# An expert's largest weight over the partitions: two small TensorE products and a VectorE maximum in place of a POOL instruction

## The chip, the cores and the metric

The kernel runs on one core of a Trainium2 chip. The metric is the device time of one execution in microseconds. Before the change three runs gave 1509.94, 1512.34 and 1515.03 us; the median is 1512.34 us. One more execution was profiled; all rows below come from it.

## The reference

A batch of 8 sequences of 2496 tokens with 256 channels goes through a spectral filter and then through a mixture of eight experts, of which each token uses the one with the largest logit:

```python
X = np.fft.rfft(x, axis=1)
y = np.fft.irfft(X * F[None], n=x.shape[1], axis=1)      # F = filt_r + 1j * filt_i
x = y.reshape(B * S, D)                                   # 19968 tokens
xn = x / (np.linalg.norm(x, axis=-1, keepdims=True) + 1e-06)
en = expert_emb / (np.linalg.norm(expert_emb, axis=-1, keepdims=True) + 1e-06)
logits = xn @ en.T / tau
expert_idx = np.argmax(logits, axis=1)                    # and gate_w, its softmax weight
for e in range(E):
    mask = expert_idx == e
    h = np.maximum(x[mask] @ w1[e], 0.0)                  # 256 -> 1024
    out[mask] = gate_w[mask, None] * (h @ w2[e])          # 1024 -> 256
```

## The kernel before

Each of the eight sequences is one group. Its filter is a two-step Fourier transform written as products on TensorE. `conv_s1` (names `in`, `s`) multiplies the loaded tokens, scratch `SD` in DRAM takes the result; `conv_s2` loads it back (`a`), transforms (`s`), multiplies by the filter (`yy` and `xs` on VectorE, lines 458 and 460), adds the two on POOL (line 494, from the second group on) and transforms back (`sa`), into scratch `ZD`; `conv_sb` loads `ZD`, makes the tokens (`y`), turns them into two half-precision parts (`rows`), transposes them (`tp`), takes the logits (`lp`), and routes. Routing works on chunks of four steps (eight 128-row pieces; the last chunk of a group has six): VectorE finds the expert, TensorE counts the rows ahead (`rk`, line 682), VectorE makes the target indices (`ixi`, line 704), and POOL scatters each piece to its expert's area of `XS` (line 711, one indirect DMA a piece, 22 pieces a group).

An expert's block of 256 rows (a slot) loads its rows transposed (`xT`, line 834, on SP's queue), multiplies them by the expert's first weights (`ph`, line 865), makes `h` on ScalarE and VectorE (lines 871 and 872), multiplies by the second weights (`po`, line 892), and scatters the result (line 900, POOL). A slot of group g can start only when all 22 pieces of group g are scattered. Eight slots, one an expert, are run for each group while the next group's filter runs between their products; in the end 33 blocks of 128 rows take the rows that are left.

The weights are prepared once, while the first group's filter runs: for each expert e and each of its two matrices, VectorE takes the largest absolute value of each partition (`largest`, lines 239 to 243, name `wmax`), POOL spreads the maximum over the partitions (`spread_max`, line 246, name `wall`), VectorE turns it into a power of two (`scales`, lines 248 to 257, name `wsc`), and ScalarE, VectorE and POOL split the scaled weights into two half-precision parts (`halves`, lines 259 to 272; POOL's part is line 269). Experts 0 to 6 take both matrices in one call, expert 7 takes them in two calls, since its raw weights lie where expert 6's were: nine calls of `spread_max` in all. `prep` steps this work: 0.6 of a step for each step of the first group (`PREP_AT`, `PREP_RATE`), and one for each call of `spread` after that.

What sets the order: in the first group (the head, everything up to the first slot) TensorE's and ScalarE's instructions stand in the order of the code. A scheduler orders all the others, and everything behind the head, by its own timeline; each engine then runs its list strictly in order. The small tiles of TensorE's results share pools: `ps_c` has two buffers, which `s`, `sa`, `tp` and `rk` take in turn.

Of the kernel before, what the change touches and what calls it, by code (L numbers as in the profile page):

```python
# [13 lines left out]
F32 = mybir.dt.float32  # L14
F32R = mybir.dt.float32r
I32 = mybir.dt.int32
AF = mybir.ActivationFunctionType
ALU = mybir.AluOpType
AX = mybir.AxisListType
# [4 lines left out]
P = 128  # L24
# [7 lines left out]
E = 8  # L32
# [24 lines left out]
def moe_spectral_kernel(  # L57
# [16 lines left out]
    nc = tc.nc  # L74
# [12 lines left out]
    const = ctx.enter_context(tc.tile_pool(name="const", bufs=1))  # L87
# [14 lines left out]
    ps_c = ctx.enter_context(tc.tile_pool(name="ps_c", bufs=2, space=PSUM))  # L102
# [18 lines left out]
    ident = const.tile([P, P], F16, tag="ident", name="ident")  # L121
# [2 lines left out]
    nc.vector.tensor_copy(lt16, lt32)  # L124
    one16 = const.tile([P, P], F16, tag="one16", name="one16")
    nc.vector.memset(one16, 1.0)


    w8i = const.tile([P, E], I32, tag="w8i", name="w8i")
# [66 lines left out]
    isc = const.tile([P, E], F32, tag="isc", name="isc")  # L196

    wmax = const.tile([P, E, 2], F32, tag="wmax", name="wmax")
    wall = const.tile([P, E, 2], F32, tag="wall", name="wall")
    wsc = const.tile([P, E, 2], F32, tag="wsc", name="wsc")  # L200
    winv = const.tile([P, E, 2], F32, tag="winv", name="winv")
    wmx = const.tile([P, 4], F32, tag="wmx", name="wmx")
# [2 lines left out]
    def weight_load(q, e, j):  # L205

        w = (w1, w2)[j]
        if e + 1 < E:
            raw = W32[:, e + 1, j * 2048:(j + 1) * 2048]
            q.dma_start(raw, w[:, e])  # L210
            raws[e, j] = [[raw[:, i * 1024:(i + 1) * 1024]] for i in range(2)]
        elif j == 0:
            raw = W32[:, e, 2048:4096]
            q.dma_start(raw, w[:, e])
            raws[e, j] = [[raw[:, i * 1024:(i + 1) * 1024]] for i in range(2)]
        else:
            raw = W32[:, e, 2048:3072]
            q.dma_start(raw, w[:, e, 1024:2048])
            small = []
            for i in range(2):  # L220
                t = mp2.tile([P, 512], F32, tag="wp", name=f"wraw{i}")
                q.dma_start(t, w[:, e, i * 512:(i + 1) * 512])
                small.append(t)
            raws[e, j] = [small, [raw]]
# [10 lines left out]
    def weight_halves():  # L235

        v = nc.vector

        def largest(e, j):
            pieces = raws[e, j][0] + raws[e, j][1]  # L240
            for i, r in enumerate(pieces):
                v.tensor_reduce(out=wmx[:, i:i + 1], in_=r, axis=AX.X, op=ALU.max, apply_absolute_value=True)
            v.tensor_reduce(out=wmax[:, e, j:j + 1], in_=wmx[:, :len(pieces)], axis=AX.X, op=ALU.max)

        def spread_max(e, js):
            nc.gpsimd.partition_all_reduce(wall[:, e, js], wmax[:, e, js], P, bass.bass_isa.ReduceOp.max)

        def scales(e, js):
            v.tensor_scalar(out=wall[:, e, js], in0=wall[:, e, js], scalar1=2.0 ** -100, scalar2=None, op0=ALU.max)
            v.tensor_scalar(out=wsc[:, e, js].bitcast(I32), in0=wall[:, e, js].bitcast(I32), scalar1=0x7F800000,  # L250
                            scalar2=0x7F800000, op0=ALU.bitwise_and, op1=ALU.bitwise_xor)
            for j in range(js.start, js.stop):
                v.tensor_scalar(out=wsc[:, e, j:j + 1], in0=wsc[:, e, j:j + 1], scalar1=2.0 ** (13 if j else 5),
                                scalar2=None, op0=ALU.mult)
            v.reciprocal(winv[:, e, js], wsc[:, e, js])
            if js.stop == 2:
                v.tensor_tensor(out=isc[:, e:e + 1], in0=winv[:, e, 0:1], in1=winv[:, e, 1:2], op=ALU.mult)

        def halves(e, j):
            sc = wsc[:, e, j // 2:j // 2 + 1]  # L260
            pieces = raws[e, j // 2][j % 2]
            w = 1024 // len(pieces)
            for i, raw in enumerate(pieces):
                hi = W[:, e, j * 2048 + i * w:j * 2048 + (i + 1) * w]
                lo = W[:, e, j * 2048 + 1024 + i * w:j * 2048 + 1024 + (i + 1) * w]
                if j == 0:
                    nc.scalar.activation(raw, raw, AF.Copy, scale=sc)
                    nc.scalar.copy(hi, raw)
                    nc.gpsimd.tensor_tensor(out=lo, in0=raw, in1=hi, op=ALU.subtract)
                else:  # L270
                    nc.scalar.activation(hi, raw, AF.Copy, scale=sc)
                    v.scalar_tensor_tensor(out=lo, in0=raw, scalar=sc, in1=hi, op0=ALU.mult, op1=ALU.subtract)

        def maxima(e):
            for j in range(2):
                largest(e, j)
                if j:
                    spread_max(e, slice(0, 2))
                yield

        yield from maxima(0)
        for e in range(E - 1):
            if e + 1 < E - 1:
                yield from maxima(e + 1)
            scales(e, slice(0, 2))
            for j in range(4):
                halves(e, j)
                if j == 3:
                    prepped[0] = e + 1
                yield  # L290
        e = E - 1
        for j, order in ((0, (0, 1)), (1, (3, 2))):
            yield
            weight_load(nc.sync, e, j)
            yield
            yield
            largest(e, j)
            spread_max(e, slice(j, j + 1))
            yield
            scales(e, slice(j, j + 1))  # L300
            for k in order:
                halves(e, k)
                yield
        prepped[0] = E
# [800 lines left out]
```

## Time and profile before

| what | value |
|---|---|
| three runs, median | 1512.34 us (1509.94 to 1515.03) |
| profiled execution | 1499.08 us |
| its span, first to last instruction | 1497.2 us |
| mean granted TensorE clock, as a share of 2.4 GHz | 0.924 |
| busy: TensorE | 1301.8 us, 87% |
| busy: VectorE, ScalarE, POOL | 873.5, 693.7, 548.7 us |
| the nine POOL reductions | 3.3 us busy |

Busy time says how long instructions ran on an engine, not whether anybody waited for it. The span is 1.9 us shorter than the execution's own time. The profiled execution is 13 us (0.9%) faster than the median of the three runs, so a sum made in it is carried over as a difference.

### The profile page before, as it was taken

What the parts mean: (1) busy time and instruction counts of PE and PEld (TensorE: products, weight loads), DVE (VectorE), ACT (ScalarE), POOL (GpSimd) and SP (SyncE); (2) the same over time, 40 slices, a digit from 0 to 9 for tenths busy, and PEclk for the clock granted to TensorE, in tenths of its full rate; (3) what the DMA queues carried; (4) which work ended last, traced back from release to release, by engine and by line L of the source; (5) the groups of instructions that cost most, each with busy time, mean ns of one, the idle gap of its engine ahead of it and who ended that gap; (6) DMA issues with size and microseconds to landing.
All of it is one profiled execution on the core that took longest, in us unless ns stands there. A gap on an engine that the chain in (4) does not pass through costs nothing.

```text
span 1497.2 us, 31982 instructions
## 1 busy us (share of the span) xinstructions
PE 1301.8 (87%) x10956; PEld 988.2 (66%) x10956; DVE 873.5 (58%) x2841; ACT 693.7 (46%) x1578; POOL 548.7 (37%) x614
## 2 busy tenths in 40 slices
PE   5644557998997998899979988997999789999997
PEld 1212235766765776686658666865787578899997
DVE  2558765563474757575648555664658432266664
ACT  2435554543562665375437634662665122333332
POOL 0021454245524543552445254525433431222222
PEclk7876678999998999999989999999999889999999
DMA  8865375646774775577457746674753222122211
GB/s 273 302 213 200 118 211 158 187 133 189 215 188 130 205 217 156 166 220 183 140 166 201 195 121 185 195 192 124 200 169 92 76 67 54 50 49 48 49 45 40
DMA packets 230494, 229.16 MB, mean 153 GB/s; under 512 B 126089, under 2 KB 172497, under 8 KB 228405
## 3 DMA queue, kind: packets, MB, share of 16 engines
q1 hardware_dynamic: 200908, 151.93, 37.7%
q0 software_dynamic: 26400, 60.07, 12.8%
q10 hardware_dynamic: 3017, 15.02, 3.0%
q8 instruction: 92, 1.51, 0.4%
q14 instruction: 77, 0.63, 0.1%
HBM read 121.61 MB, written 84.84 MB: 138 GB/s over the span
## 4 chain that ended last, share of the span: by engine, by line
PE 61%; issue 15%; POOL 3%; DMA 2%; ACT 1%; DVE 1%; another core or an unknown queue 1%; POOLq 0%; SPq 0%; ACTq 0%; DVEq 0%
PE po L892 22%; PE ph L865 21%; PE y L403 5%; PE s L403 5%; POOL out_dram L900 3%; PE tp L606 2%; PE sa L408 2%; PE s L408 2%; DMA f<-ZD 1%; PE lp L621 1%; PE sa L512 1%; DMA ZD<-z 1%; DVE xs L460 0%; DMA f<-in_filt 0%
## 5 line engine op out<-in xcount | busy, mean ns | idle before, releaser
L892 PE MATMUL po<-W,h 128*128 128x256 f16 (+1 forms) x3864 | 519.8, 279 | 27.9 <-issue 27.5
L892 PEld LDWEIGHTS <-h 128*128 128x128 f16 x3864 | 375.5, 100 | 132.4 <-issue 85.3
L865 PE MATMUL ph<-xT,W 128*128 128x256 f16 x3072 | 414.8, 279 | 30.9 <-issue 18.7
L872 DVE SCALAR_TENSOR_TENSOR h<-ph,h 128x512 f16<-128x512 f32 (+1 forms) x388 | 232.0, 598 | 277.6 <-ACT h L871 240.6
L865 PEld LDWEIGHTS <-W 128*128 128x128 f16 x3072 | 300.1, 100 | 129.0 <-issue 91.4
L871 ACT ACTIVATE h<-ph 128x512 f16<-128x512 f32 (+1 forms) x388 | 203.4, 525 | 378.8 <-PE ph L865 205.4
L900 POOL DMA_INDIRECT out_dram<-o,meta x161 | 171.5, 1065 | 359.0 <-ACT o L899 319.4
L711 POOL DMA_INDIRECT XS<-rows,ixi x176 | 176.6, 1004 | 172.4 <-issue 136.2
L403 PE MATMUL y<-f,csb_sb 120*128 120x512 f32 (+1 forms) x192 | 101.2, 612 | 39.8 <-DVE rows L562 17.7
L494 POOL TENSOR_TENSOR yy<-yy,xs 128x512 f32<-128x512 f32 x70 | 94.3, 1349 | 109.1 <-DVE xs L460 69.5
L363 POOL DMA_DIRECT2D in<-in_x x84 | 66.9, 797 | 154.9 <-PE s L403 113.4
L403 PE MATMUL s<-in,c_sb 117*128 117x512 f32 (+1 forms) x192 | 111.1, 672 | 12.8 <-DMA in<-in_x 8.1
L865 PE MATMUL ph<-xT,wp 128*128 128x128 f16 x1584 | 104.9, 219 | 0.2
L865 PEld LDWEIGHTS <-wp 128*128 128x128 f16 x1584 | 96.7, 98 | 3.2 <-issue 0.7
L587 ACT ACTIVATE rows<-y 128x256 f16<-128x256 f32 x176 | 66.0, 384 | 64.7 <-PE y L403 58.8
L559 ACT ACTIVATE rows<-y,rr 128x256 f16<-128x256 f32 x176 | 73.9, 473 | 46.8 <-DVE rr L592 44.7
L426 ACT COPY s<-s 128x512 f32<-128x512 f32 x88 | 51.5, 586 | 91.4 <-PE s L403 43.5
L458 DVE TENSOR_TENSOR yy<-s,f 128x256 f32<-128x256 f32 x160 | 60.9, 419 | 52.5 <-ACT xs L487 39.4
L562 DVE SCALAR_TENSOR_TENSOR rows<-y,rr,rows 128x256 f16<-128x256 f32 x176 | 77.1, 478 | 22.5 <-ACT rows L559 19.8
L853 DVE COPY wp<-W 128x1024 f16 x132 | 62.1, 471 | 45.3 <-PE ph L865 44.8
L899 ACT ACTIVATE o<-po,meta 128x256 f32<-128x256 f32 x161 | 69.4, 475 | 34.2 <-PE po L892 26.7
L460 DVE SCALAR_TENSOR_TENSOR xs<-xs,sgn_sb,f 128x256 f32<-128x256 f32 x160 | 82.0, 551 | 0.0
(170 smaller groups left out, 1397.0 us busy)
## 6 DMA issues: line engine op xcount, KB each, us to landing
f<-in_filt SPq DMA_DIRECT2D x160, 256.0 KB
a<-SD SPq DMA_DIRECT2D x80, 256.0 KB
ZD<-z SPq DMA_DIRECT2D x80, 256.0 KB
SD<-s SPq DMA_DIRECT2D x80, 240.0 KB
f<-ZD SPq DMA_DIRECT2D x80, 240.0 KB
in<-in_x POOLq DMA_DIRECT2D x70, 234.0 KB
W<-in_w ACTq DMA_DIRECT2D x14, 1024.0 KB
XS<-rows,ixi POOLq DMA_INDIRECT x176
```

The source lines that it names most:

```text
L403: nc.tensor.matmul(out_, c[:a.shape[0]], a, start=True, stop=True)
L460: nc.vector.scalar_tensor_tensor(out=o, in0=i, scalar=sgn_sb[:, k2:k2 + 1], in1=f, op0=ALU.mult, op1=ALU.mult)
L494: nc.gpsimd.tensor_tensor(out=yy, in0=yy, in1=xs, op=ALU.add)
L559: nc.scalar.activation(rows[:, i, 0:D], y[:, i], AF.Copy, scale=rr[:, u:u + 1])
L562: nc.vector.scalar_tensor_tensor(out=rows[:, i, D:2 * D], in0=y[:, i], scalar=rr[:, u:u + 1], in1=rows[:, i, 0:D], op0=ALU.mult, op1=ALU.s ...
L711: i = nc.gpsimd.indirect_dma_start(out=XS, out_offset=bass.IndirectOffsetOnAxis(ap=ix, axis=0), in_=src, in_offset=None)
L865: last["pe"] = nc.tensor.matmul(ph[:, fi, :size], wp[:, k * 2 + wh, fi * P:(fi + 1) * P], xT[:, xh * 2 + k], start=(c == 0), stop=(c == 5))
L871: nc.scalar.activation(h[:, 0, :, :size], ph[:, :, :size], AF.Relu)
L872: hd = nc.vector.scalar_tensor_tensor(out=h[:, 1, :, :size], in0=ph[:, :, :size], scalar=0.0, in1=h[:, 0, :, :size], op0=ALU.max, op1=ALU. ...
L892: nc.tensor.matmul(self.po[:, s], self.hs[fp][:, hh, fi, s * P:(s + 1) * P], self.Wp[:, off + wh * 1024:off + wh * 1024 + D], start=(fp == ...
L899: nc.scalar.activation(o, self.po[:, s], AF.Copy, scale=self.meta[:, s, 1:2])
L900: i = nc.gpsimd.indirect_dma_start(out=out, out_offset=bass.IndirectOffsetOnAxis(ap=self.meta[:, s, 0:1].bitcast(I32), axis=0), in_=o, in_ ...
```

## The change

`spread_max` no longer uses POOL. VectorE first bounds the per-partition maxima from below and masks them to their exponents (these two steps stood in `scales` before). TensorE multiplies them by a 128x128 identity, which lays the 128 partitions' values along one row in a PSUM tile `pm`; VectorE takes the maximum of that row (`wtop`) and puts it on a 2x2 diagonal (`wdg`); a second product with a matrix of ones brings it to all 128 partitions, and VectorE flips the exponent into the scale `wsc`. The tile `pm` comes from the pool `ps_c`. Two constants, `ident32` and `one32`, are made at the start.

```diff
+    ident32 = const.tile([P, P], F32, tag="ident32", name="ident32")
+    nc.vector.tensor_copy(ident32, ident)
+    one32 = const.tile([2, P], F32, tag="one32", name="one32")
+    nc.vector.memset(one32, 1.0)
...
         def spread_max(e, js):
-            nc.gpsimd.partition_all_reduce(wall[:, e, js], wmax[:, e, js], P, bass.bass_isa.ReduceOp.max)
+
+            n = js.stop - js.start
+            m = wmax[:, e, js]
+            v.tensor_scalar(out=m, in0=m, scalar1=2.0 ** -100, scalar2=None, op0=ALU.max)
+            v.tensor_scalar(out=m.bitcast(I32), in0=m.bitcast(I32), scalar1=0x7F800000, scalar2=None,
+                            op0=ALU.bitwise_and)
+            pm = ps_c.tile([P, 2, P], F32, tag="c", name=f"pm{e}_{js.start}")
+            nc.tensor.matmul(pm[:n, 0], m, ident32, start=True, stop=True)
+            v.tensor_reduce(out=wtop[:n, e:e + 1], in_=pm[:n, 0], axis=AX.X, op=ALU.max)
+            v.tensor_scalar(out=wdg[:n, e, :n], in0=ident32[:n, :n], scalar1=wtop[:n, e:e + 1], scalar2=None,
+                            op0=ALU.mult)
+            nc.tensor.matmul(pm[:, 1, :n], one32[:n], wdg[:n, e, :n], start=True, stop=True)
+            v.tensor_scalar(out=wsc[:, e, js].bitcast(I32), in0=pm[:, 1, :n].bitcast(I32), scalar1=0x7F800000,
+                            scalar2=None, op0=ALU.bitwise_xor)
 
         def scales(e, js):
-            v.tensor_scalar(out=wall[:, e, js], in0=wall[:, e, js], scalar1=2.0 ** -100, scalar2=None, op0=ALU.max)
-            v.tensor_scalar(out=wsc[:, e, js].bitcast(I32), in0=wall[:, e, js].bitcast(I32), scalar1=0x7F800000,
-                            scalar2=0x7F800000, op0=ALU.bitwise_and, op1=ALU.bitwise_xor)
```

The change also alters what the scheduler does with the rest. The line numbers of the changed kernel are 4 higher before the edit, and 15 higher behind it (711 becomes 726).

POOL, the last chunk of the first group's filter, before. `ISA` is the instruction that changes POOL's configuration, the second one is the reduction of expert 6 itself, `XS` rows are the scatters:

```order
L363 DMA in_10_1064<-in_x 117x256
L363 DMA in_10_1064<-in_x 39x256
L246 ISA
L246 ISA wall<-wmax 128x2
L596 ISA
L596 IOTA rows_10_1078 128x2
L711 DMA XS<-rows_0_584,ixi_0_967 178304x258 x2
L711 DMA XS<-rows_1_621,ixi_0_967 178304x258 x2
```

The same place in the changed kernel:

```order
L284 TENSOR_TENSOR W<-W 128x1024
L726 DMA XS<-rows_0_608,ixi_0_999 178304x258 x2
L726 DMA XS<-rows_1_643,ixi_0_999 178304x258 x2
L726 DMA XS<-rows_2_670,ixi_0_999 178304x258 x2
L726 DMA XS<-rows_3_699,ixi_0_999 178304x258 x2
L611 IOTA rows_9_1064 128x2
L378 DMA in_10_1096<-in_x 117x256
```

The three `ISA` rows are gone here as everywhere, and the first eight scatters stand directly behind the `W` step.

TensorE, from the last routing step of the first group (`rk0_8`) to its first slot (`ph0_0`), before; between `s2_1_0` and the slot stand five more filter products of the second group:

```order
L682 MATMUL rk0_8_1321<-oh0_8_1316,lt16_138 128x48
L403 MATMUL s2_1_0_1456<-a1_0_1427,c2_sb_118 128x512
L403 MATMUL s2_1_1_1495<-a1_1_1429,c2_sb_118 128x512
L403 MATMUL s2_1_2_1532<-a1_2_1431,c2_sb_118 128x512
L512 MATMUL sa_1_0_1565<-yy1_0_1461,m1_sb_119 128x512
L403 MATMUL s2_1_3_1572<-a1_3_1454,c2_sb_118 128x512
L512 MATMUL sa_1_1_1599<-yy1_1_1500,m1_sb_119 128x512
L865 MATMUL ph0_0_0_1401<-xT0_0_1397,W_201 128x256
```

The same place in the changed kernel, with the pair of expert 6 ahead of it and the first product of expert 7 behind the slot's first 24 products:

```order
L258 MATMUL pm6_0_1343<-ident32_142,wmax_207 2x128
L262 MATMUL pm6_0_1343<-wdg_209,one32_144 128x2
L697 MATMUL rk0_8_1365<-oh0_8_1360,lt16_138 128x48
L418 MATMUL s2_1_0_1496<-a1_0_1467,c2_sb_118 128x512
L880 MATMUL ph0_0_0_1441<-xT0_0_1437,W_205 128x256
L880 MATMUL ph0_0_1_1473<-xT0_0_1437,W_205 128x256
L258 MATMUL pm7_0_1534<-ident32_142,wmax_207 1x128
L418 MATMUL s2_1_1_1542<-a1_1_1469,c2_sb_118 128x512
```

Five filter products have moved from ahead of the first slot to between the slots' products.

TensorE, from the last routing step of the second group (`rk1_8`) to that group's first slot (`ph1_0`), before; rows of one tile are shown once:

```order
L682 MATMUL rk1_8_3100<-oh1_8_3075,lt16_138 128x48
L865 MATMUL ph0_6_3_3186<-xT0_6_2777,W_201 128x256
L892 MATMUL po0_6_3169<-W_201,h0_6_0_3017 128x256
L865 MATMUL ph0_7_0_3218<-xT0_7_3088,W_201 128x256
L865 MATMUL ph0_7_1_3264<-xT0_7_3088,W_201 128x256
L865 MATMUL ph0_7_2_3312<-xT0_7_3088,W_201 128x256
L403 MATMUL s2_2_0_3332<-a2_0_3284,c2_sb_118 128x512
L865 MATMUL ph0_7_3_3377<-xT0_7_3088,W_201 128x256
L892 MATMUL po0_7_3347<-W_201,h0_7_0_3231 128x256
L865 MATMUL ph1_0_0_3427<-xT1_0_3273,W_201 128x256
```

The same place in the changed kernel:

```order
L697 MATMUL rk1_8_3150<-oh1_8_3125,lt16_138 128x48
L880 MATMUL ph0_7_2_3362<-xT0_7_3138,W_205 128x256
L418 MATMUL s2_2_0_3382<-a2_0_3334,c2_sb_118 128x512
L880 MATMUL ph0_7_3_3427<-xT0_7_3138,W_205 128x256
L907 MATMUL po0_7_3397<-W_205,h0_7_0_3281 128x256
L527 MATMUL sa_2_0_3472<-yy2_0_3387,m1_sb_119 128x512
L418 MATMUL s2_2_3_3495<-a2_3_3380,c2_sb_118 128x512
L527 MATMUL sa_2_1_3510<-yy2_1_3417,m1_sb_119 128x512
L880 MATMUL ph1_0_0_3477<-xT1_0_3323,W_205 128x256
```

Before, 132 slot products and 3 filter products stand between the two; in the changed kernel 73 slot products and 6 filter products. From the third group's slots on, the two orders are nearly the same.

## Rows read from the trace of the kernel before

**Rows 1.** The page, busy us (share of the span) of each engine.
```profile
PE 1301.8 (87%) x10956; PEld 988.2 (66%) x10956; DVE 873.5 (58%) x2841; ACT 693.7 (46%) x1578; POOL 548.7 (37%) x614
```

**Rows 2.** Stretches: from:to, length, busy us of each engine, TensorE clock, DMA, GB/s.
```profile
0.00:187.20 187.20, 98.86 (x331) 41.86 (x331) 116.05 (x347) 77.53 (x153) 37.28 (x57) 0.73 0.68 221
187.20:212.95 25.75, 10.45 (x20) 3.67 (x21) 17.55 (x38) 14.34 (x19) 20.87 (x17) 0.59 0.76 224
212.95:262.00 49.05, 38.77 (x240) 26.39 (x240) 26.73 (x57) 22.27 (x36) 16.36 (x15) 0.90 0.56 164
262.00:1497.20 1235.20, 1153.69 (x10369) 916.26 (x10367) 713.14 (x2401) 579.53 (x1372) 474.16 (x526) 0.96 0.51 141
```

**Rows 3.** Waits of PE from 262 us on: us in total, times, longest.
```profile
PE ph L865 <- DVE h L872: 4.5, 3, 2.0
```

**Rows 4.** Line 246, POOL's reduction: durations in ns min/median/max, first and last start.
```profile
L246 POOLq MODIFY_POOL_CONFIG  x14: 1/36/37, 2.1 to 232.7; - x14
L246 POOL PARTITION_ALL_REDUCE wall<-wmax x9: 351/371/377, 36.1 to 239.6; - x9
```

**Rows 5.** POOL's timeline: start, us, engine, line, operation [idle before <-releaser].
```profile
163.35 0.37 POOL L246 PARTITION_ALL_REDUCE wall<-wmax  x1 [6.78 <-issue]
170.51 0.13 POOL L596 IOTA rows<- 128x2 int32 x1 [6.79 <-issue]
...
182.09 2.13 POOL L269 TENSOR_TENSOR W<-W 128x1024 f16<-128x1024 f32 x1
...
204.65 0.90 POOL L711 DMA_INDIRECT XS<-rows,ixi  x1 [0.30 <-issue]
...
251.87 1.25 POOL L494 TENSOR_TENSOR yy<-yy,xs 128x512 f32<-128x512 f32 x1 [7.85 <-DMA ZD<-z]
...
332.63 0.99 POOL L711 DMA_INDIRECT XS<-rows,ixi  x1 [6.68 <-issue]
...
341.63 0.98 POOL L711 DMA_INDIRECT XS<-rows,ixi  x1 [0.30 <-issue]
...
354.01 0.89 POOL L711 DMA_INDIRECT XS<-rows,ixi  x1 [0.30 <-issue]
```

**Rows 6.** DVE's timeline, the indices and what waits for the reduction.
```profile
163.75 0.17 DVE L249 TENSOR_SCALAR wall<-wall 128x2 f32<-128x2 f32 x1 [3.21 <-POOL wall L246]
...
179.55 0.34 DVE L704 CAST ixi<-ix 128x1 int32<-128x1 f32 x4
...
188.10 0.20 DVE L690 TENSOR_REDUCE ix<-l 128x6 f32<-128x48 f32 x1
...
240.01 0.15 DVE L249 TENSOR_SCALAR wall<-wall 128x1 f32<-128x1 f32 x1 [5.09 <-POOL wall L246]
```

**Rows 7.** PE's timeline, from the last routing step to the first slots, and at 241.
```profile
187.20 0.22 PE L682 MATMUL rk<-oh,lt 128*128 128x48 f16 x1 [5.31 <-DVE oh L674]
...
206.90 2.08 PE L512 MATMUL sa<-yy,m_sb 128*128 128x512 f32 x2 [12.11 <-POOL yy L494]
...
212.95 2.78 PE L865 MATMUL ph<-xT,W 128*128 128x256 f16 x24 [0.76 <-DMA xT<-XS]
...
241.01 1.44 PE L865 MATMUL ph<-xT,W 128*128 128x256 f16 x6 [4.35 <-DVE wsc L253]
```

**Rows 8.** PE's timeline, from the second group's routing to its first slot.
```profile
329.38 0.19 PE L682 MATMUL rk<-oh,lt 128*128 128x64 f16 x1
...
339.71 0.19 PE L682 MATMUL rk<-oh,lt 128*128 128x48 f16 x1
...
357.83 1.88 PE L403 MATMUL s<-a,c_sb 128*128 128x512 f32 x4
359.55 1.47 PE L865 MATMUL ph<-xT,W 128*128 128x256 f16 x12
```

**Rows 9.** SP's queue, the loads of the two groups' first slots.
```profile
209.65 1.35 SPq L834 DMA_TRANSPOSE xT<-XS  x1
...
356.22 1.24 SPq L834 DMA_TRANSPOSE xT<-XS  x1
```

More of the change, by code (lines that the diff above doesn't have):

```diff
@@ L198, in moe_spectral_kernel @@
     wmax = const.tile([P, E, 2], F32, tag="wmax", name="wmax")
-    wall = const.tile([P, E, 2], F32, tag="wall", name="wall")
+    wtop = const.tile([2, E], F32, tag="wtop", name="wtop")
+    wdg = const.tile([2, E, 2], F32, tag="wdg", name="wdg")
     wsc = const.tile([P, E, 2], F32, tag="wsc", name="wsc")
```

## The prediction

> **What bounds the kernel now.** I read the page's busy times first: TensorE is busy 87% of the span, no other engine over 58% [rows 1]. The table of stretches says where the missing 13% lie [rows 2]. From 262 us to the end TensorE is busy 1153.7 of 1235.2 us at a granted clock of 0.96, and its longest wait for another engine there, as the list of waits has it, sums to 4.5 us [rows 3]: the products themselves are the time. Before the first slot (0 to 212.95 us) it is busy 109 of 213 us, at clocks of 0.73 and 0.59 between the levels of 1.2 and 2.4 GHz; from there to 262 us it is busy 38.8 of 49.05 at 0.90. So a microsecond that TensorE no longer idles before 262 us ends the kernel a microsecond earlier, unless it idles again later. The change acts between 36 and 241 us, where the nine reductions stand [rows 4].
>
> The view of line 246 shows 0.37 us for a reduction, 3.3 us for nine. The timeline of POOL shows the rest of the price [rows 5]: it changes its configuration before and after (14 such instructions), and sits idle 6.8 us before the reduction at 163.35 and 6.8 us before the next instruction at 170.51, with no other releaser. One reduction thus takes POOL out for 13.9 us. Who waits then? VectorE, whose list has the maximum ahead of other work: 3.2 us at 163.75 and 5.1 us at 240.01 [rows 6], and through it TensorE 4.35 us at 241.01 [rows 7]. And whatever POOL has behind it: the 22 scatters of the first group, of which the first run only after 170.5 and the last at 204.65, though the second chunk's indices are there from 179.55 on and the third's from 188.3 [rows 5, 6]. The first slot needs all of them: its load goes out at 209.65, its first product runs at 212.95 [rows 7, 9].
>
> **The change part by part.** The sum is made in the profiled execution (1499.08 us, 1.9 more than its span) and carried over as a difference to the median of 1512.34.
>
> POOL's part goes: all nine reductions with their configuration changes, as the order shows. *Scatters:* the first eight now stand directly behind a weight step and can run when their indices are ready, ahead of the second chunk. The second eight start at 179.55 or just after; eight scatters start within 9.0 us of each other (332.63 to 341.63 [rows 5]), 1.29 us each, so they take 10.3 us, to 189.9. A weight step (2.13 us at 182.09) follows, to 192.0, then six scatters, 7.7 us, to 199.7. Before, the end was at 204.65 + 0.90 = 205.55. Allowing half a microsecond for gaps: -5.4. Were the indices alone the limit (188.3 + 0.5 + 7.7 = 196.5) it would be -9; were POOL's wait only replaced by another, 0.
>
> *The pairs.* Seven pairs of products (experts 0 to 6) come into the head's fixed order. A pair holds TensorE from the first product to the end of the second, since the second needs VectorE's maximum and diagonal. No row shows such a product; the nearest is a pair of 512-column fp32 passes, 2.08 us at the half clock (at 206.90 [rows 7]), a quarter of which is 0.5 for 128 columns. VectorE's maximum I take as the 0.20 of a small reduction, the diagonal as 0.17 [rows 6], the second product and the hand-overs as 0.2: 1.1 us. Below, it costs nothing where TensorE idles anyway (88 of the head's 187 us [rows 2]); above, 2.5 us where VectorE has a step of routing between the two. I take half of seven at 1.1 as uncovered: +4.0. VectorE has five small steps an expert for two, 3 x 0.17 x 7 = 3.6 us in a stretch where it is busy 116 of 187; that is in the +4.0. Against it stands the 3.2 us at 163.75, which lies in the routing chain and goes: -3.2. Net +0.8. The two pairs of expert 7 stand between slot products, apart from each other: +0.5 for the passes. The constants are made in the first microseconds under the loads: 0. The pair's tile takes a buffer of `ps_c`, which lets the next filter product wait for the one before; the uncovered half holds that.
>
> The Trainium skill, GPSIMD Engine Reference, section "Engine selection", sends a reduction along the partitions to GPSIMD and not to VectorE. The trace disagrees in its price, not in its instruction: 0.37 us of work, 13.9 of absence. By that rule the sum would have only the costs of the pairs in it and the kernel would be slower; the sum goes by the rows.
>
> *The first slot moves ahead of filter work.* Before, six filter products of the second group run between `rk0_8` and the slot; now one does. Five products run later, where TensorE is full. One costs 0.86 us at full clock, half of 359.55 - 357.83 [rows 8]: +4.3.
>
> *From 212.95 to 262 us* TensorE idles 10.3 us, and the clock of 0.90 (a fifth of the stretch at the half level) takes up to 4.9 more [rows 2]: 15.2. Behind it are POOL's absences at 218 and 239.6 us: VectorE's waits, the 4.35 us of TensorE, and the additions that POOL owes the filter (the one at 251.87 came 7.85 us late [rows 5]). I let 5 of the 15.2 stand, because VectorE still waits for the load of expert 7's weights there: -10. Bounds: -4 (only the wait of 4.35 goes) and -14.
>
> *What is late next: the second group's first slot.* By the order, the second group's filter now lags its slots. In rows 8 and 9 the way from the second chunk's routing to that slot is: 329.38 to the first scatter 332.63, 3.25; eight scatters 10.3; two result scatters 2.6; six scatters 7.7; 1.3 to the load at 356.22; 3.3 to the product at 359.55: 28.5 us. Before, TensorE's own work between took 30.2 (329.38 to 359.55): covered, with nothing to spare. In the new order there lie between 143 slot products at 0.109 us (12 more take 1.31 us: 2.78 - 1.47 [rows 7, 8]), six filter products and two loads' worth of `s`, and one microsecond of small ones: 15.6 + 5.2 + 1.7 + 1.0 = 23.5. TensorE comes up to 5.0 us early, less gaps (before: 30.2 against 27.0 of work by the same prices, 3.2), and comes out of the wait at the half clock: +4. Bounds 0 and +7.
>
> Sum: -5.4 + 0.8 + 0.5 + 4.3 - 10 + 4 = **-5.8 us**: 1493.3 in the profiled execution's time, 1506.5 against the median.
>
> **The rivals.**
> *More comes through.* The scatters follow the indices (-9 in place of -5.4), and gaps cover the seam (0 in place of +4): -13.4, 1499. For it: POOL is free, the third chunk's indices were 16 us early. Against: the second batch and the weight step are in POOL's list ahead of the third.
> *It is given back.* Expert 7's maximum reaches TensorE's list: its product stands between slot products and waits for a load that VectorE waits for now. Then 10 of the 15.2 stand, not 5: -0.8, 1511.5. For it: both loads of expert 7 are issued only when expert 6 and then its own first half are done. Against: VectorE's wait for the reduction is what TensorE felt there.
> *Slower: the pairs decide.* The head's order is fixed, so each of the seven pairs holds up what TensorE has behind it, and VectorE's list puts routing steps between a pair's maximum and its diagonal: 7 x 2.5 = 17.5 in place of 4.0, a difference of 13.5, so +7.7, 1520. It decides once the last routing step `rk0_8` is later than about 191 us (187.2 before [rows 7]), since from then on the third batch waits for its indices and no longer for POOL. For it: TensorE's half clock in the head and VectorE's 62% there. Against: the 88 idle us.
> That POOL keeps its configuration changes is out: the order has none left between the start and the end.
>
> **How the numbers follow.** Runs of this kernel spread by 0.3% (4.5 us); less than that is "same". The forecast has a chance of 0.44 with a range of its own of -11 to -1, two thirds of it below -4.5; more comes through 0.17; given back 0.22; slower 0.17. Faster: 0.29 + 0.17, and a little of the third, 0.47; same: 0.15 + 0.20, 0.35; slower 0.18. The range takes in -16 and +8: the first with most of the second case, the last with half of the fourth: 1496 to 1520.
>
> **What would show it.** Right, step by step: no configuration change on POOL before the tail; the first scatter near 162 and the last near 200; the first slot's product near 208.5; no wait of VectorE for POOL of 3 to 5 us; TensorE's idle time in the 50 us from the first slot down from 10 to some 4; a wait of some 4 us at `sa_2_0` or `ph1_0_0`. Wrong: `rk0_8` later than 191 (the pairs), a first slot after 213, TensorE waiting at the products of expert 7, or a seam of more than 8 us.

## The result, and the profile after: slower by 0.64%

The changed kernel takes 1518.11 us (median of 20 runs, 1509.37 to 1523.43); the kernel before, run beside it, 1506.95 us (20 runs). The ratio is 1.0064, 95% interval 1.0046 to 1.0082: about 10 us slower, where 5.8 us faster was forecast. In two later sets of runs, each beside the kernel before, the ratio was 1.0019 (0.9991 to 1.0047) and 1.0033 (1.0013 to 1.0052). The profiled execution took 1519.78 us, span 1518.0. The one profiled of before (1499.08 us) was as fast as the fastest of its 20 runs, so the 20.8 us between the two spans are nearly twice what the kernels differ by; places are read from the profiles here, sizes from the ratios.

The page's busy times; POOL, relieved of nine reductions, is hardly less busy than in [rows 1], since what it lost was idle time:

```profile
PE 1315.9 (87%) x10992; PEld 995.4 (66%) x10992; DVE 872.2 (57%) x2870; ACT 695.7 (46%) x1578; POOL 545.3 (36%) x605
```

The stretches of [rows 2], same columns:

```profile
0.00:187.20 187.20, 106.39 (x342) 45.43 (x342) 112.46 (x335) 73.08 (x146) 32.29 (x47) 0.71 0.69 218
187.20:212.95 25.75, 6.65 (x26) 2.86 (x26) 17.73 (x61) 14.05 (x16) 20.64 (x17) 0.50 0.63 188
212.95:262.00 49.05, 44.39 (x310) 32.16 (x310) 31.39 (x72) 25.64 (x42) 18.13 (x15) 0.93 0.66 182
262.00:1518.00 1256.00, 1158.51 (x10317) 914.91 (x10315) 710.65 (x2403) 582.92 (x1374) 474.20 (x528) 0.95 0.52 139
```

TensorE is busy 44.4 us of the third stretch (38.8 before). The 4.7 us that it idles there all lie before its first slot, which comes at 217.61: from then to 262 us it does not idle at all, at a granted clock of 0.97. It is busier before 187 us too, by 7.5 us, and yet later. PE's timeline shows it, against [rows 7]:

```profile
173.03 0.58 PE L258 MATMUL pm<-ident,wmax 128*2 128x128 f32 x2
175.57 0.58 PE L262 MATMUL pm<-wdg,one 2*128 2x2 f32 x2 [1.96 <-issue]
176.08 2.08 PE L418 MATMUL s<-in,c_sb 117*128 117x512 f32 x2
...
184.09 0.23 PE L697 MATMUL rk<-oh,lt 128*128 128x64 f16 x1 [4.87 <-DVE oh L689]
...
190.22 0.59 PE L258 MATMUL pm<-ident,wmax 128*2 128x128 f32 x2
191.77 0.58 PE L262 MATMUL pm<-wdg,one 2*128 2x2 f32 x2 [0.97 <-DVE se L711]
192.78 0.22 PE L697 MATMUL rk<-oh,lt 128*128 128x48 f16 x1 [0.43 <-DVE rows L714]
...
217.61 4.08 PE L880 MATMUL ph<-xT,W 128*128 128x256 f16 x24 [18.82 <-DMA xT<-XS]
```

Between a pair's two products TensorE stands still; the pair of expert 5 holds it from 173.03 to 176.15, 3.1 us. `rk0_8` comes at 192.78 (187.20 before), past the 191 that the prediction set as the sign of its third rival, and the first slot's product at 217.61 (212.95). VectorE's timeline says why the pair takes so long:

```profile
174.13 0.28 DVE L259 TENSOR_REDUCE wtop<-pm 2x1 f32<-2x128 f32 x1 [0.37 <-PE pm L258]
174.34 0.85 DVE L577 SCALAR_TENSOR_TENSOR rows<-y,rr,rows 128x256 f16<-128x256 f32 x2
175.12 0.20 DVE L667 TENSOR_TENSOR l<-l,lp 128x64 f32<-128x64 f32 x1
175.25 0.26 DVE L260 TENSOR_SCALAR wdg<-ident,wtop 2x2 f32<-2x2 f32 x1
175.38 0.15 DVE L605 TENSOR_SCALAR q<-ssq 128x2 int32<-128x2 int32 x1
...
176.19 0.16 DVE L263 TENSOR_SCALAR wsc<-pm 128x2 int32<-128x2 int32 x1
```

Work on the tokens (L577) and on routing (L667) stands in VectorE's list between the pair's maximum and its diagonal. On POOL the first batch of scatters starts at 163.53 as forecast, against the 170.5 after the reduction in [rows 5]; the later ones do not keep the lead:

```profile
163.53 1.07 POOL L726 DMA_INDIRECT XS<-rows,ixi  x1 [3.12 <-DVE ixi L719]
...
188.42 1.09 POOL L726 DMA_INDIRECT XS<-rows,ixi  x1 [5.25 <-DVE l L666]
...
200.61 2.13 POOL L284 TENSOR_TENSOR W<-W 128x1024 f16<-128x1024 f32 x1
202.93 1.00 POOL L726 DMA_INDIRECT XS<-rows,ixi  x1 [0.19 <-issue]
...
209.91 0.88 POOL L726 DMA_INDIRECT XS<-rows,ixi  x1 [0.30 <-issue]
```

The second batch waits 5.25 us for VectorE and starts at 188.42, where 179.55 was forecast, and the last scatter ends at 210.79, not 199.7 (205.55 before). At the seam to the second group, against [rows 8]:

```profile
340.05 0.19 PE L697 MATMUL rk<-oh,lt 128*128 128x64 f16 x1
...
354.32 0.20 PE L697 MATMUL rk<-oh,lt 128*128 128x48 f16 x1 [1.13 <-issue]
...
375.53 0.71 PE L880 MATMUL ph<-xT,W 128*128 128x256 f16 x5 [2.61 <-DMA xT<-XS]
```

From the first slot to this product, `ph1_0_0`, it is 157.9 us. For before, [rows 8] end too early: the product at 359.55 is the last tile of the first group's expert 7 (`ph0_7_3`). Counted by the order, with 132 slot products and three filter products (four, then two of the passes of `s`) behind `rk1_8`, `ph1_0_0` is the product at 364.35, the first row here. In the kernel before run again (`e9` below), the second row, the product at that place waits for the slot's load:

```profile
364.35 1.36 PE L865 MATMUL ph<-xT,W 128*128 128x256 f16 x11
351.47 1.36 PE L865 MATMUL ph<-xT,W 128*128 128x256 f16 x11 [0.99 <-DMA xT<-XS]
```

So before it was 151.4 us, and the changed kernel takes 6.5 us more from its first slot to this place.

### The profile page after: what moved, and what is told of

Same layout as the page of the kernel before. It is cut to its first block, busy times and chain, and to the rows that moved or that the text cites. A ratio compares the mean times of both kernels' runs of the same rounds, so it can differ in the third digit from the quotient of the medians.

```text
span 1518.0 us, 32029 instructions
## 1 busy us (share of the span) xinstructions
PE 1315.9 (87%) x10992; PEld 995.4 (66%) x10992; DVE 872.2 (57%) x2870; ACT 695.7 (46%) x1578; POOL 545.3 (36%) x605
## 4 chain that ended last, share of the span: by engine, by line
PE 64%; issue 16%; DMA 8%; POOL 4%; DVE 4%; ACT 2%; another core or an unknown queue 1%; POOLq 0%; SPq 0%; ACTq 0%; DVEq 0%
PE ph L880 21%; PE po L907 21%; PE s L418 6%; PE y L418 5%; POOL out_dram L915 3%; DMA f<-ZD 2%; PE tp L621 2%; PE s L423 2%; PE sa L423 2%; PE sa L527 2%; DMA W<-in_w 1%; POOL XS L726 1%; PE lp L636 1%; DVE wmx L247 1%; DMA SD<-s 1%
## 5 line engine op out<-in xcount | busy, mean ns | idle before, releaser
L880 PE MATMUL ph<-xT,W 128*128 128x256 f16 x3072 | 421.5, 281 | 51.1 <-issue 26.0
L577 DVE SCALAR_TENSOR_TENSOR rows<-y,rr,rows 128x256 f16<-128x256 f32 x176 | 77.1, 477 | 20.9 <-ACT rows L574 19.1
L623 DVE COPY yT<-tp 128x1024 f16<-128x1024 f16 x88 | 60.3, 685 | 47.8 <-remote 22.1
```

The source lines that it names most:

```text
L577: nc.vector.scalar_tensor_tensor(out=rows[:, i, D:2 * D], in0=y[:, i], scalar=rr[:, u:u + 1], in1=rows[:, i, 0:D], op0=ALU.mult, op1=ALU.s ...
L880: last["pe"] = nc.tensor.matmul(ph[:, fi, :size], wp[:, k * 2 + wh, fi * P:(fi + 1) * P], xT[:, xh * 2 + k], start=(c == 0), stop=(c == 5))
```

## The experiments

Two theories stood at the start. *Order*: expert 7's products change TensorE's order, so that the second group's routing step `rk1_0` stands behind 540 slot products and not 444, and that costs the time. *Pairs*: TensorE, which works in order, stands still inside the pairs in the head. The experiments ran in five sets (`e1` to `e4`, `e5` to `e8`, `e9` to `e12`, `e13` to `e16`, `e17` and `e18`), and the sets differ: before's median was 1495 us in the first, 1507 in the second and 1405 to 1406 in the others. So each ratio is to the runs of before in the same set.

**Head or tail alone.** In `e1` (and `e16`) expert 7 stays on POOL, in `e2` experts 0 to 6 do:

```
 def spread_max(e, js):
+    if e == E - 1:          # e1, e16;  e2: if e < E - 1
+        nc.gpsimd.partition_all_reduce(wall[:, e, js], wmax[:, e, js], P, ReduceOp.max)
+        return
     ...
```

Expected of `e1`: 

> Experts 0 to 6 spread by the two products, expert 7 (two of the nine calls) by POOL's reduction as before; TensorE's order is then that of before, with seven pairs more in the head. Theory order (the loss comes from where the scheduler puts the filter products and group 1's ranks once expert 7 goes over TensorE: rk1_0 stands behind 540 slot products instead of 444): this kernel is within 0.3% of before, 1503 to 1508 us against 1507, first scatter near 163, rk1_8 no later than 344. Theory pairs (TensorE is held 1.6 to 3.1 us per pair in the head, and the first slot is late by it): 1511 to 1516 us, first slot product after 216.

Expected of `e2`: 

> Experts 0 to 6 by POOL's reduction, expert 7 alone by the products; TensorE's order from the first slot on is then that of the changed kernel (rk1_0 behind 540 slot products). Theory order: as slow as the changed kernel or nearly, 1512 to 1518 us against 1507; first slot product 212 to 214, rk1_8 352 or later, ph1_0_0 370 or later. Theory pairs: 1504 to 1509 us, since only two of nine pairs are left and these stand where TensorE waited for POOL.

Measured: `e1` 1.0092 (1.0058 to 1.0126), `e2` 0.9998 (0.9974 to 1.0022). The whole loss comes with the head's pairs (`e1` is above the ranges of both theories); my favourite, the order, fell as the only cause. But `e2` shows that expert 7's part holds a gain and a loss. The stretch from 212.95 to 262 us in `e2`:

```profile
212.95:262.00 49.05, 49.05 (x340) 34.93 (x339) 30.35 (x71) 29.40 (x49) 19.75 (x17) 0.99 0.65 193
```

TensorE idles no more there (10.3 us before), at a clock of 0.99 for 0.90, and the kernel is no faster: something gives it back later.

**No spreading.** `e3` (again as `e18`) and, for experts 0 to 6 alone, `e10`:

```
-    nc.gpsimd.partition_all_reduce(wall[:, e, js], wmax[:, e, js], P, ReduceOp.max)
...
-    v.tensor_scalar(out=wall[:, e, js], in0=wall[:, e, js], scalar1=2.0 ** -100, ...)
+    v.tensor_scalar(out=wall[:, e, js], in0=wmax[:, e, js], scalar1=2.0 ** -100, ...)
```

Expected of `e3`: 

> No maximum over the partitions at all: each partition takes the exponent of its own largest weight (left out: POOL's nine reductions, and no products in their place). TensorE's order is that of before. Both theories: faster than before, since nothing is added; this is the most that the change could have given: 1497 to 1503 us against 1507 (first scatter 9 us and last scatter 5 us earlier, first slot product at 206 to 209). If it comes out at 1505 to 1509, the scatters' head start was worth nothing in the end, and the prediction's first term falls.

Expected of `e10`: 

> Experts 0 to 6 take each partition's own largest weight (left out: their maximum over the partitions), expert 7 by POOL's reduction as before. No products are added, TensorE's order is before's: this is the gain of the head by itself (scatters free of POOL's configuration change, no VectorE wait). As predicted for the head: 5 us, first slot at 207 to 209, ratio 0.995 to 0.998. Rival: the ranks on TensorE set the scatters as soon as POOL is out of the way, so first slot 209 to 212, ratio 0.998 to 1.001. e1_head_products less this one is the price of seven pairs in the head.

Measured: `e3` 0.9933 (0.9905 to 0.9961), `e10` 0.9974 (0.9952 to 0.9996). With nothing in its place, POOL's work is worth 0.7% and the head's share of it 0.3%: 10 and 4 us. The place that `e10` was to show was missed: its first slot came at 215.71, not at 207 to 209. But the first `y` product of the head came at 105.44 in that profile and at 98.94 in `e9`, before again, ahead of any routing; so a single profile's first slot says little of the pairs.

**Pairs taken apart.** In `e4` the second product is issued one step of the head later, so that other products lie between:

```
-    nc.tensor.matmul(pm[:, 1, :n], one32[:n], wdg[:n, e, :n], start=True, stop=True)
-    v.tensor_scalar(out=wsc[:, e, js].bitcast(I32), in0=pm[:, 1, :n].bitcast(I32), ...)
+    later.append((e, js))
+def spread_back():          # at the start of the next step
+    while later:
+        e, js = later.pop()
+        ...
+        pb = ps_c.tile([P, 2], F32, tag="c", name=f"pb{e}_{js.start}")
+        nc.tensor.matmul(pb[:, :n], one32[:n], wdg[:n, e, :n], start=True, stop=True)
+        v.tensor_scalar(out=wsc[:, e, js].bitcast(I32), in0=pb[:, :n].bitcast(I32), ...)
```

Expected: 

> The changed kernel with each pair taken apart: first product, reduce and diagonal in one step of the head, second product one step later with a PSUM tile of its own, so TensorE has other work between them. rk1_0 stands behind 508 slot products (540 in the changed kernel, 444 before). Theory pairs: the holds go, 1508 to 1512 us, first slot product near 214. Theory order: 1513 to 1518 us, first slot a few us earlier than 217.6 but rk1_8 350 or later.

Measured: 1.0019 (0.9995 to 1.0044), `rk0_8` at 187.4, first slot at 212.5. Most of the head's loss goes, but not all of the kernel's.

**The order restored.** Why does the order change? My reading: the pair's tile takes its turn in `ps_c`, whose two buffers the filter products use; expert 7's weights land late, so the filter products behind that turn wait, and the scheduler puts slot products ahead of them. Between the first group's `y` and the second's, `ps_y` is idle:

```
-    pm = ps_c.tile([P, 2, P], F32, tag="c", name=f"pm{e}_{js.start}")
+    pool, tag = (ps_y, "y") if e == E - 1 else (ps_c, "c")      # e7: else (ps_h, "h")
+    pm = pool.tile([P, 2, P], F32, tag=tag, name=f"pm{e}_{js.start}")
```

`e5` is that and nothing else; `e7` moves the head's pairs to `ps_h` as well; `e8` is `e5` with the pairs taken apart as in `e4`, `e6` is `e7` with them taken apart. In all four `rk1_0` is back behind 444 to 450 slot products.

Expected of `e5`: 

> The changed kernel, with expert 7's two pairs in a PSUM tile of ps_y (which is idle until group 1's y products) in place of ps_c, whose two buffers the filter products rotate through. TensorE's order is then that of before again (rk1_0 behind 444 slot products). Theory order at the seam (the changed kernel gains 6 to 10 us after its first slot and gives it back because rk1_0 to rk1_8 stand 10 us later): first slot as late as in the changed kernel (216 to 218), but TensorE over 90% busy from there to 262 and ph1_0_0 no later than 362; ratio to before 0.997 to 1.001 (the changed kernel: 1.0064). Rival (the order costs nothing, the gain is lost again elsewhere, as to the clock): 1.004 to 1.008.

Expected of `e6`: 

> Both cures: the pairs of experts 0 to 6 taken apart over two steps, in tiles of ps_h (idle in the head), those of expert 7 in ps_y. Theory (head holds plus order make the whole loss): first slot product at 209 to 213, ph1_0_0 at 350 or earlier, ratio to before 0.991 to 0.996, near the kernel without any spreading (0.9933). Rival (the products themselves and their VectorE work cost, however they are placed): 0.998 to 1.004.

Expected of `e7`: 

> As e5_last_in_psy, and the pairs of experts 0 to 6 in ps_h, but not taken apart: first product, wait for VectorE, second product back to back on TensorE. Theory hold (TensorE, in order, stands still between a pair's two products): like e5_last_in_psy within 0.2%, first slot 215 to 218. Theory rotation (the pair takes one of the two buffers of ps_c from the filter products): the head is regained, first slot 209 to 213, ratio 0.992 to 0.996.

Expected of `e8`: 

> The pairs taken apart but still in ps_c for experts 0 to 6, expert 7 in ps_y: e4_split_pair with the order of before. Theory hold: 0.992 to 0.997, first slot 210 to 214. Theory rotation: no better than e5_last_in_psy, first slot 215 to 218. Theory order at the seam: 4 to 9 us faster than e4_split_pair's ratio of 1.0019.

Measured: `e5` 0.9996 (0.9978 to 1.0013), `e6` 0.9961 (0.9936 to 0.9986), `e7` 0.9999 (0.9974 to 1.0025), `e8` 0.9966 (0.9946 to 0.9985). The order costs 0.7% (changed kernel to `e5`), the standing still 0.3% to 0.4% (`e5` to `e8`, `e7` to `e6`), and which PSUM pool the head's pairs use costs nothing that shows (`e5` to `e7`, `e8` to `e6`). Both theories hold, each for its part. The 0.3% to 0.4% are barely clear of the intervals here; later sets give more (0.5%, 1.0%).

**The pair doubled, and the kernels again.** `e11` makes each of the seven pairs of `e1` twice:

```
+    for _ in range(2):
         pm = ps_c.tile([P, 2, P], F32, tag="c", name=f"pm{e}_{_}")
         ...
```

Expected of `e11`: 

> e1_head_products with the pair of each of experts 0 to 6 made twice, one after the other (the second repeats the first's numbers): seven pairs more on TensorE, in order, each with its wait for VectorE. Theory hold, at 5 to 10 us for seven pairs: 1.013 to 1.017 against 1.0092. If pairs in the head were covered by idle TensorE, as the prediction took for over half of their time: 1.008 to 1.012.

Expected of `e9`: 

> The kernel before, unchanged, for a profile on the same chip as the next three. Of the others so far, the stretch from 400 us to the end took 1094 to 1100 us in the first four experiments and 1109 to 1117 us in the second four, the chip being another each time. If that is the chip and not the kernels, before's stretch here is within 4 us of that of the three beside it, and its ratio is 0.998 to 1.002. If early gains are given back later (by the clock, say), before's late stretch is 8 to 15 us shorter than that of the kernels that reach 400 us earlier.

Expected of `e12`: 

> The changed kernel again, for a profile on the same chip as before's. All theories: ratio 1.004 to 1.009, first slot product 4 to 8 us later than in e9_before_again, TensorE's busy time in the 50 us behind the first slot 4 to 8 us above that of before, and ph1_0_0 another 8 to 12 us later against the first slot.

Measured: `e11` 1.0186 (1.0155 to 1.0217), `e9` 1.0003 (0.9981 to 1.0026), `e12` 1.0019 (0.9991 to 1.0047), less than the 1.004 expected at the least. PE's timeline in `e11`, the pairs of one expert back to back:

```profile
156.63 0.59 PE L262 MATMUL pm<-ident,wmax 128*2 128x128 f32 x2
157.95 0.58 PE L266 MATMUL pm<-wdg,one 2*128 2x2 f32 x2 [0.73 <-DVE wdg L264]
158.46 0.58 PE L262 MATMUL pm<-ident,wmax 128*2 128x128 f32 x2
159.67 0.58 PE L266 MATMUL pm<-wdg,one 2*128 2x2 f32 x2 [0.62 <-DVE wdg L264]
```

A pair with nothing in its way takes 1.8 us at the half clock (158.46 to 160.25), 1.16 of it products. Seven more cost 1.0% against `e16`, 14 us or 2.0 us each: of a second pair, nothing shows as covered by TensorE's idle time.

**Four in one set.**

Expected of `e13`: 

> The changed kernel once more, beside e14 to e16 on one chip. If its loss is the sum of its parts as measured so far, 1.004 to 1.008 on a chip with a granted clock of 0.92, and it lies 0.5% to 0.9% above e15. If the loss depends on the chip's clock, 1.000 to 1.004 on a chip near 0.95.

Expected of `e14`: 

> e6_split_free_psum once more: 0.993 to 0.998, the fastest of the four; against e15 at least 0.2% faster (the hold of unsplit pairs).

Expected of `e15`: 

> e5_last_in_psy once more (unsplit pairs, before's order restored): 0.998 to 1.002 if the order's 0.7% is real, the same as e13 within 0.3% if it is not.

Expected of `e16`: 

> e1_head_products once more (products for experts 0 to 6, POOL for 7): 1.007 to 1.012 if the interaction is real, so above the changed kernel itself; 1.002 to 1.006 if the price of seven pairs is the 0.6% of e5 against e3 less the 0.26% that the scatters gain.

Measured: `e13` (the changed kernel) 1.0033, `e15` (order restored) 0.9982 (0.9962 to 1.0002), `e14` (taken apart as well) 0.9932 (0.9910 to 0.9954), `e16` (head alone) 1.0086 (1.0059 to 1.0114). PE's timeline of `e13`, unsplit, from the first `y` product to the first routing step:

```profile
101.51 2.08 PE L418 MATMUL y<-f,csb_sb 120*128 120x512 f32 x2 [7.55 <-DMA f<-ZD]
...
147.00 0.58 PE L258 MATMUL pm<-ident,wmax 128*2 128x128 f32 x2
148.32 0.59 PE L262 MATMUL pm<-wdg,one 2*128 2x2 f32 x2 [0.73 <-DVE wdg L260]
148.84 2.08 PE L418 MATMUL s<-in,c_sb 117*128 117x512 f32 x2
...
157.40 0.24 PE L697 MATMUL rk<-oh,lt 128*128 128x64 f16 x1 [5.43 <-DVE oh L689]
```

and of `e14`, taken apart:

```profile
101.68 2.08 PE L433 MATMUL y<-f,csb_sb 120*128 120x512 f32 x2 [8.71 <-DMA f<-ZD]
...
146.27 0.58 PE L261 MATMUL pm<-ident,wmax 128*2 128x128 f32 x2
146.78 2.08 PE L433 MATMUL s<-in,c_sb 117*128 117x512 f32 x2
148.65 0.97 PE L636 MATMUL tp<-ident,rows 128*128 128x128 f16 x8
...
149.73 0.38 PE L274 MATMUL pb<-wdg,one 2*128 2x2 f32 x2
...
151.76 0.20 PE L712 MATMUL rk<-oh,lt 128*128 128x64 f16 x1 [1.65 <-DVE oh L704]
```

Two pairs lie in this way (one is not shown), which takes 55.9 us in `e13` and 50.1 in `e14`. It is the surest sign of the hold: 54.9 to 57.4 us in all eight executions with the seven pairs unsplit in the head (59.0 in `e11`), 47.8 to 50.7 in all eleven with none or with pairs taken apart. So not taking a pair apart costs nearly 3 us there, more than the 1.9 that TensorE is held; that routing goes back and forth between TensorE and VectorE, so that each turn starts later, would explain it, but was not tested by itself. Ahead of this way, where three of the seven pairs stand, no such price shows: its first product comes on average at 102.6 us in the eight and at 101.8 in the eleven (100.7 to 105.2, and 98.7 to 105.4).

The seam, in `e13` and then in `e15`:

```profile
339.26 0.19 PE L697 MATMUL rk<-oh,lt 128*128 128x48 f16 x1
...
359.12 2.29 PE L880 MATMUL ph<-xT,W 128*128 128x256 f16 x13 [2.96 <-DMA xT<-XS]
```

```profile
327.14 0.19 PE L698 MATMUL rk<-oh,lt 128*128 128x48 f16 x1
...
345.80 1.36 PE L881 MATMUL ph<-xT,W 128*128 128x256 f16 x11 [1.32 <-DMA xT<-XS]
```

With first slots at 212.91 and 217.31, `ph1_0_0` comes 146.2 us and 128.5 us later. Of the 17.7 between them, 24 slot products (2.6 us at 0.109) and eight filter products (6.9 us at 0.86) are work that stands in this way in the changed order alone; 8.2 are lost. Five of the eight stood ahead of the first slot in `e15`, where TensorE waits anyway, so their 4.3 us are lost too; against that, the first slot of `e13` is 4.4 us earlier. That leaves 8.1 us by these two profiles; the ratios say 0.5%, 7 us.

**What was still open.** `e17` is `e16` with the pairs taken apart, in `ps_h`:

Expected of `e17`: 

> e16_head_products_again (experts 0 to 6 by products, 7 by POOL) with the seven pairs taken apart and put in ps_h, as in e6. If standing still inside a pair is the whole price: as e10_head_unspread, 0.995 to 1.000. If the products and VectorE's five further instructions per expert cost too: 1.002 to 1.007.

Expected of `e18`: 

> e3_no_spread once more (left out: every maximum over the partitions): 0.990 to 0.995. If it is no faster than e14_split_again's 0.9932, nine pairs taken apart cost nothing that can be measured; if it is 0.988 or less, they cost 0.5%.

Measured: `e17` 0.9982 (0.9960 to 1.0003), `e18` 0.9883 (0.9856 to 0.9909). Taking the pairs apart gives 1.0%, all that the seven cost between `e10` and `e16` (1.1%). By `e18` the nine pairs of `e14`, though taken apart, still cost 0.5%; by `e3` and `e6`, 0.3%, which the intervals do not tell from nothing.

## Why the prediction was wrong

The parts add up along a chain of kernels, from each to the next: `e3`, `e6`, `e5`, the changed kernel in the earlier sets, and `e18`, `e14`, `e15`, `e13` in the later ones. The differences of their ratios, taken of 1507 and of 1406 us (by the intervals of two ratios, each is known to within 4 to 6 us):

| Part | Predicted, us | Measured, us |
|---|---|---|
| POOL's reductions go (scatters -5.4, VectorE's wait -3.2, start stretch -10) | -18.6 | -10 (`e3`), -16 (`e18`) |
| nine pairs, taken apart | +4.5 for this and the next | +4, +7 |
| TensorE standing still inside them | | +5, +7 |
| order: displaced products +4.3, seam +4 | +8.3 | +10, +7 |
| Sum | -5.8 | +10, +5 |

*The step that failed is the size of the pairs*: "I take half of seven at 1.1 as uncovered: +4.0", and 0.5 for expert 7's. They cost 9 to 14 us. Both factors were wrong. The duration: 1.5 to 3.1 us in the changed kernel's head, because VectorE's steps on tokens and routing stand between maximum and diagonal, and because the second product, 2 columns wide, takes as long as the first. The cover: little. The seven pairs hold TensorE 14.5 us in the changed kernel's head, doubled they cost all that they take (`e11`), and only the three ahead of the first `y` product show no price. Of TensorE's 88 idle us in before's head 45 end with a step of VectorE and 29 with a load from DRAM; where routing runs from TensorE to VectorE and back, what delays one link delays the next, whether or not TensorE is idle on average. This was the third rival in its mechanism, and its chance of 0.17 was too low; that its total of +7.7 was near is partly luck, since it had the pairs at 17.5 (9 to 14) and POOL's part at -18.6 (-10 to -16), and the two errors cancel. What I had held against it, the idle time, is a share over the stretch.

*A second term was too large*: POOL's part, -18.6 in the sum, is -10 by `e3` (6 to 14 by its interval) and -16 by `e18` (13 to 20). In the earlier sets it missed by more than the pairs did (8.5 us against 5.0), in the later ones by less (2.2 against 9.4). With pairs and order at their measured cost, even the full -18.6 would have left the change 1 to 3 us slower.

*Scatters.* The first batch went early as forecast. The second waited for its indices, not for POOL, since `rk0_4` came at 184.09 (175.62 before): the gain of -5.4 assumed indices as early as before. Without pairs the head does gain, 4 us by `e10`, against the 8.6 of scatters and VectorE's wait.

*The start stretch* gained at least what was forecast. In the fixed window TensorE has 5.6 us more in the changed kernel, 10.3 in `e2`; counted from each kernel's own first slot, its idle time goes from 10.3 us to none in both, where the sum let 5 us of lost time stand. Expert 7's two pairs hold nothing there, because slot products stand between their two products.

*The order* came out near its size, 7 to 10 for 8.3, but partly by luck. Its cause was not understood: I put it down to the first slot moving ahead, and `e5` shows that it is one tile's turn in a pool of two. And the seam was worked out from a wrong row: TensorE's own work from 329.38 to `ph1_0_0` was 35.0 us before (to 364.35), not 30.2. The slot's load went out at 356.22, and 3.3 to 4.2 us after such a load these profiles show the product, so before had 4 to 5 us to spare where I had written "nothing to spare".

*The rule set beside the sum.* The Trainium skill, GPSIMD Engine Reference, section "Engine selection", would have kept the reduction on GPSIMD. The changed kernel is slower, as by that rule, but for another reason: `e6` and `e14` do the same products, placed otherwise, and beat before by 0.4% and 0.7%; the measurement speaks against the rule here.

*Open.* `e16`, the head's pairs alone, is slower than the changed kernel; the seven pairs cost 1.0% where expert 7 stays on POOL (`e16` to `e17`) and 0.5% where it doesn't (`e15` to `e14`). In the profiles of `e16` and `e17` the first slots are 5.8 us apart, not 14.6; where the rest is lost was not found. Nor was it shown why the changed kernel loses 0.64% in one set of runs and 0.2% to 0.3% in two others.

## What to carry to other kernels

A small product whose partner waits for VectorE can cost an in-order TensorE the whole round trip, and idle time of TensorE does not cover it when that idle time is itself a wait in the same chain: issue the second half a step later, with other products between. A tile that waits for late data must not take its turn in a pool that running work rotates through; the cost appears far away, as an order that the scheduler changed. And price what is taken away by leaving it out: `e3` and `e18` put the gain at 10 and 16 us, against the 18.6 of the sum.

## What the runs showed of the hardware that was not expected

The width of a tiny fp32 product hardly mattered. Each product is two passes; in the changed kernel a pass of the 2-column product has a median of 348 ns, one of the 128-column product 371:

```profile
L258 PE MATMUL pm<-ident,wmax x18: 269/371/421, 66.2 to 248.8; 128*2 128x128 f32 x14, 128*1 128x128 f32 x4
L262 PE MATMUL pm<-wdg,one x18: 245/348/369, 67.4 to 252.2; 2*128 2x2 f32 x14, 1*128 1x1 f32 x4
```

Sets of runs differ by more than any of these changes: the kernel before takes 1495 to 1507 us in the earlier ones and 1405 to 1406 in the three later ones. The stretch of [rows 2] from 262 us to the end, in `e9`, before in a later set:

```profile
262.00:1402.20 1140.20, 1106.13 (x10355) 901.53 (x10353) 708.32 (x2399) 580.03 (x1370) 474.91 (x525) 0.99 0.56 152
```

The granted clock there is 0.99 for 0.96. TensorE's idle time that ends with no releaser ("issue"), from 262 us on, is 27.5 and 18.7 us before the two large groups of slot products in the profile of before shown first, and 62.4 in all; in `e9` there is none. The prediction, which called the products themselves the time there, passed over it. First `e9`, then before:

```profile
L892 PE MATMUL po<-W,h 128*128 128x256 f16 (+1 forms) x3768 | 486.1, 274 | 0.0
L865 PE MATMUL ph<-xT,W 128*128 128x256 f16 x2942 | 380.7, 274 | 13.6 <-DVE h L872 6.4 <-DMA xT<-XS 5.3 <-DVE ixi L704 1.8
```

```profile
L892 PE MATMUL po<-W,h 128*128 128x256 f16 (+1 forms) x3770 | 507.8, 279 | 27.9 <-issue 27.5 <-ACT h L871 0.2
L865 PE MATMUL ph<-xT,W 128*128 128x256 f16 x2952 | 397.7, 279 | 23.8 <-issue 18.7 <-DVE h L872 4.5 <-DVE se L696 0.6
```

Up to the first slot the two agree within 4 us at every mark compared. The same divide runs through all twenty profiles, whatever the kernel: 58 to 71 us of such idle time in the ten of the earlier sets, none in the ten from `e9` on. What makes it was not shown. It need not be the chip: the first and the last set bear the same chip number, and before took 1495 us in one and 1405 in the other. A microsecond count does not carry from one set of runs to another; even the changed kernel's ratio went from 1.0064 to 1.0019.
